# A four-tap filter on TensorE: from shifted 128-row products to products on 32-row groups, four at once, with the weights built in one operation

## The chip, the cores and the metric

One core of one Trainium2 chip. The metric is the time of one execution on the device in microseconds. The kernel before ran three times: 268.84, 270.32 and 270.63 us, median 270.32. The engines are called by the profile's names: PE (TensorE matmuls), PEld (its weight loads), DVE (VectorE), ACT (ScalarE), POOL (GpSimd) and SP (the queue that issues nearly all transfers).

## The reference

Two independent layers whose outputs stand side by side. Layer A (columns 0 to 639 of the output) is the one that the change touches; its first step is a causal filter of four taps over the 2048 positions, one filter for each of the 640 channels, and a product with v:

```python
k_pad = jnp.pad(k, ((0, 0), (ks - 1, 0), (0, 0)))
for t in range(ks):                       # ks = 4
    k_shift = k_shift + k_pad[:, t:t + S, :] * shift_k[:, ks - 1 - t][None, None, :]
kv = k_shift * v
...
y_f = kv_f * kf_f[None, :, :, :]          # a long convolution with ssm_k, by FFT
y = irfft2(y_f)[:S] + kv * ssm_D
return q * y
```

Layer B is an attention of 32 heads of 20 over four segments of 512, with a memory carried from segment to segment: projections of x by wq, wk and wv, softmax inside the segment, a linear term from the memory, and a projection by wo. All inputs are bf16.

## The kernel before

Layer A goes by slices of 128 channels: `conv(dp)` for dp 0 to 4. Its long convolution is a Fourier transform written as matmuls (`spectrum`, with the table Wf), complex products on DVE (`product`) and the inverse as matmuls (`inverse`, with Wi). Layer B goes by eight units, a segment's half of the heads each: `project(u)` makes keys, queries and values, `attend(u)` fills blocks of logits (matmuls on 32-row groups, one head per group and PSUM bank, then two exponentials on ACT over two banks each, into the tile ET), multiplies by the values and divides.

`short_filter` (lines 476 to 528) makes k_shift * v of one slice. A transposing DMA brings k as kr, channels on partitions and positions along the row (line 492). For each of the four banks b the filter is a sum of matmuls into one PSUM bank: the stationary operand is kr read at every eighth position, 128 channels x 128 positions, and the moving operand is a piece of skd, which holds for each tap a diagonal matrix of that tap's weights. The result has positions on partitions and channels along the row, as `spectrum` wants it, and one DVE multiply per bank puts v on it (line 527, tile vt). There are two variants:

- dp 0 to 2 (lines 519 to 524): 128x128 diagonals, 7 matmuls a bank, for the distances 0, 1, -1, 2, -2, 3, -3, of 512 down to 128 columns.
- dp 3 and 4 (`TAP2 = (3, 4)`, lines 512 to 518): 64 channels with two taps each on the 128 rows, which needs copies of kr shifted by two positions. Three SBUF-to-SBUF transfers make them (lines 493 to 498, tiles kb and kr); then 10 matmuls a bank, of 128 or 64 columns.

The weights skd are built in the constructor (lines 349 to 360): the taps are brought to the right partitions by 12 tiny matmuls (lines 341 to 347), and since `SKA` names all five slices, ACT then multiplies an identity by each tap, four instructions a slice, twenty in all.

Nothing here is issued in the order of the Python text. Every call is recorded as an operation (`Recorder.add`); a stored permutation of all operations, `ORDER`, says in which order they are issued (`issue`, line 252), `BASE` gives each PSUM group its first bank of eight, and `EVICT` says for each eviction from PSUM whether DVE ("1") or ACT ("0") does it. They are made beforehand with prices as in `price` (line 198). Each engine works through its own share of the order strictly in sequence. Line 261, from which every instruction is issued, is therefore the line that the profile gives for all of them; a tile's name tells them apart (ps is PSUM, skd and kr are the filter, ET the exponentials, vt the product with v).

Of the kernel before, what the change touches and what calls it, by code (L numbers as in the profile page):

```python
# [12 lines left out]
BF16_NP = ml_dtypes.bfloat16  # L13
bf16 = mybir.dt.bfloat16
f32 = mybir.dt.float32
# [11 lines left out]
KPAD = 16  # L27
# [242 lines left out]
class Layer:  # L270
    def __init__(self, ctx, tc, A_q, A_k, A_v, A_shift_k, A_ssm_k, A_ssm_D, B_x, B_wq, B_wk, B_wv, B_wo, B_beta, out):
# [52 lines left out]
        parts = [sel_np, ml_np, mr_np, np.concatenate([np.eye(64)] * 2).astype(BF16_NP), maskbd_np, eps_np.view(BF16_NP), step_np]  # L324
# [5 lines left out]
        sel, ml, mr, id2, mb, eps, step = [pack[:, int(a):int(b)] for a, b in zip(at, at[1:])]  # L330
# [6 lines left out]
        self.taps = o2[:, 640:720].bitcast(f32).rearrange("p (n c) -> p n c", c=5) if NP else c.tile([128, 8, 5], f32, name="taps")[:]  # L337
        g = self.taps_g = self.group(1, "taps")
        tp = g.ap[:, 0, 0:40].rearrange("p (n c) -> p n c", c=5)
        sk4 = skr.rearrange("c (f p s l) -> c f s p l", f=2, p=64, s=2)  # L340
        with rec.one():
            for f in range(2):
                for l in range(2):
                    for s in range(2):
                        nc.tensor.matmul(tp[64 * s:64 * s + 64, 2 * f + l, :], lhsT=sk4[:, f, s ^ f, :, l], rhs=self.ident[0:5, 0:5], start=True, stop=True, grp=g)
            for t in range(4):
                nc.tensor.matmul(tp[:, 4 + t, :], lhsT=skr.rearrange("c (d t) -> c d t", t=4)[:, :, t], rhs=self.ident[0:5, 0:5], start=True, stop=True, grp=g)
        self.evict(self.taps, tp, g)
        self.skd = []
        for dp in range(5):  # L350
            rec.key = ("skd", dp)
            n, k, eye = (256, 64, id2) if dp in TAP2 else (512, 128, self.ident[:])
            t = c.tile([128, n], bf16, name=f"skd{dp}")
            at = 0 if dp in TAP2 else 4
            if dp in SKA:
                for i in range(4):
                    nc.scalar.activation(out=t[:, k * i:k * i + k], in_=eye, func=ACTF.Copy, scale=self.taps[:, at + i, dp:dp + 1])
            else:
                nc.vector.tensor_tensor(out=t[:].rearrange("p (t d) -> p t d", t=4), in0=eye[:, None, :].to_broadcast([128, 4, k]), in1=self.taps[:, at:at + 4, dp, None].to_broadcast([128, 4, k]), op=ALU.mult)
            self.skd.append(t[:])  # L360
# [5 lines left out]
        self.kr = c.tile([128, KPAD + S], bf16, name="kr")  # L366
# [8 lines left out]
        nc.gpsimd.memset(self.kr[:, 0:KPAD], 0.0)  # L375
        self.kb = c.tile([128, KPAD + S], bf16, name="kb")
        nc.gpsimd.memset(self.kb[:, 0:KPAD], 0.0)
# [66 lines left out]
    def conv(self, dp):  # L444
# [5 lines left out]
        def key(*k):  # L450
            rec.key = ("A", dp) + k
# [24 lines left out]
        def short_filter():  # L476
            key("lk")
            kr = self.kr
# [23 lines left out]
            if dp in TAP2:  # L502
                skd2 = self.skd[dp].rearrange("p (f l d) -> p f l d", f=2, l=2)
            else:
                skd = self.skd[dp].rearrange("p (t d) -> p t d", t=4)
            for b in range(4):
                key("ks", b)
                if b % KSW == 0:
                    g = self.group(KSW, "ks")
                ps = g.ap[:, b % KSW, :]  # L510
                first = KPAD + 1024 * (b // 2) + 4 * (b % 2)
                if dp in TAP2:
                    with rec.one():
                        for m in (0, 2, -1, 1, 3):
                            for f, kx in ((0, kr), (1, self.kb)):
                                c0, c1 = max(0, m), min(4, m + 2)
                                nc.tensor.matmul(ps.rearrange("p (c d) -> p c d", d=128)[:, c0:c1, 64 * f:64 * f + 64], lhsT=kx[:, first + m:first + m + 1017:8],
                                                 rhs=skd2[:, f, c0 - m:c1 - m, :], start=(m == 0 and f == 0), stop=(m == 3), grp=g, skip_group_check=True)
                else:
                  with rec.one():  # L520
                    for n, dl in enumerate((0, 1, -1, 2, -2, 3, -3)):
                        c0, c1 = max(0, dl), min(4, 4 + dl)
                        nc.tensor.matmul(ps[:, 128 * c0:128 * c1], lhsT=kr[:, first + dl:first + dl + 1017:8], rhs=skd[:, c0 - dl:c1 - dl, :],
                                         start=(n == 0), stop=(n == 6), grp=g, skip_group_check=True)
                if b % KSW == KSW - 1:
                    some = vt[:, b + 1 - KSW:b + 1].rearrange("p b c d -> p b (c d)")
                    V.tensor_tensor(out=some, in0=g.ap, in1=some, op=ALU.mult, grp=g)
# [388 lines left out]
    def project_out(self, s):  # L916
# [41 lines left out]
        for t in range(4):  # L958
# [29 lines left out]
KSW, IW = 1, 1  # L988
NP = 0
SKA = (0, 1, 2, 3, 4)  # L990
KQV, QN = 0, 4
TAP2 = (3, 4)
EVICT = ("10100001110000001000000010000000000000000000000000000000000000100000000000001000010001001010100110100000000000000000110000000000000010000000"
         "000000000101000100100100000000000000010000001100001000000000000000000000010110010000100")
KQW, FW, WW = 1, 1, 1
ORDER = r"""
c-jrtgMttW5Czb=Gk0=rwrjI(+um&3wry{=YqM?Jwr#$5zT#w+Y?57aNKVNmxh0R}l_(NXTtrGs6^SI}q@v`L>Jn9=NgOF7p(MXlmGV+nk_aWQR+7{bAQdE|RFeV{Sqe%KEhI&?uv8XEKCPs6rKXsuRMxIiTWU#W
Ni5MNro@oa8cWJ(eyt%v(p?H@LP;gXw2qY3G*Vw`YC~x*^`x9;k=D{uifcCs(gxB<+DZ!vEw!|<l$177TboKh=^^bTtyIx;Qc-(J9c?9bwU0EBdfH6VOM5A$9i^(ql_FAH3Tl6;p*^Lr_LjcVLCWhO=_CWBn8cG|
l3cpT2<a@brG(Vi1d>RGNJA|u4K%C_mN7C=hRY~PDPd%s43)7mTB>OyEupJ*yo{6yQb>b!gErRcx<}S%d?~3-wTaHry|PjlX$tA4$t076lL|UfR%vscB$H)|?2`~(tW#yPY?AI;N@mDL-7l?lnrzbPazK`751p$s
rL`{AHabt6X<PlJEwsHJm6qB;=W9EiC0pg7bkd&MOBZNIJtlp1wj7qux=jwrHr=jAq__6bwc16y>Kxgj+hv^|my6O*Pe`!r)M2_=FUeI|p$m1m_SY>sK(EPMiDM&lr^K~gx>YaBX_+VEb-rAYcy>mX%Pxs(6Lp|2  # L1000
kli{#<J%57FN1WCuGif%Mx$A38>fq8uP&6NwnZ+;GTo<R^{gzG!MaSA>p3~5`!%Jdv7tIdPs&n>k5rb-qT6vjpp$f(PS;a1QV(i)nXEDFzKqsUn%Ex7bD5$`WQNYv>oQeu$qKn4H|4e**2j{>?#L{CDR<?NX0{`m
!B)#reIT<n0UpU~c_nM)jjWVJc2QqQR768Uq_DTLN)jQXWwQ11L@wz&$zoUZvOblha!sE}R@)$JB{9-lcDt&lb)CGIVV1)_N-`uzY&)w@bhw?-50V5S@>DlUPCKE`^ppl7DRS8-IjK`@gq_o=Hqr)KbX?FBh#<H1
yymvg5(9ZHrp2<<_#$bM#|GIqiHSS<Q19wjNrUV9NMqr#-q4$x4!884=CeMCjkkJVze|35pg&~1^|v^9r|<QZCbzU!!0yQ}iHiZ26|XhWe##roh<JFeza^bzLT3Dx43f>p+8>!<FSMY&)C86dAM}g<laKmU$5=uO
g-@CVpS7fY(}_0DfYO#8-!(J@KeUu(fFV03SxV$U8B2wqTGkZPtgscbB38+!8&S?8ps4jjWgBJ1tcp1zA}2;$aVuf7E!YNIE_A{Wt7>5|%Vt;}6h}3yZecOgCR+*Au-qt$APa|@79Qm-5{hAt<;7g9VEIrUg;5rz
QPE0bp1ri%))xVoZ-G+BDxe(dS`jR?0jOuStPB=eJ1d3yRuBQ~U_&iG8rV8pZ0)VJ^+!WnZ(t!Tu`rCxwicUhOxeOJVyO*8SjJ%#4na$+gk`qeMxd2d!3vAYMm7kQF%-iv5-V+i4Mt;YYE8`eTZf}6R#`QWG1=V4
U>us+Sj6H6tAUL+9^n`n9j%jvXJ-qs1YB)vY^`;%C@@RNuJ%{E8LczA+g9sg|Fox7M=$Gb+pLd?ZMXRB&P42Mn=A<va|$+FKXZ#j*cR)CP!@xCFqFG3G?TI)doTinFpSB$$EKn`yJG_O+78=i1+d?0;(-0piHOKR
*2Y1L#va&ZJFN@i@{mPmEhOU^i^qHDz&^Z-!`2gZ(3L58&d%B;>&trR#*`d|RJ>xBZ5q<B7mnHt)W<P9V#n=-rDjLY#7V1*(Ku!2tv9Bl0WMlZYY68gq-AKkV4>I*H!K~S;-=lQ!3?nG7{c2Y+3uKHW8AgLxM%Hn
)goDYUbFjXg!IhJ>z0uN*pv5dEHiOAnxGj@+hWYZ1AAnT?THQIQ=5%B2xFr-kip2pUR;9VoQs9%#0;E=wFqmYxdJ1&2wC~edb2Yh+Ip<R7`8)pF2xf(w`^R7hse!w+<<3zfc6;Ayd24ie2Ud*fjnG^HCTm7e2yG!
gPhF8`MANB$j1c;L4HnV7q-F_w#6k}Mr%x^djW>>f}GAG6feZ0gim8(7Go6Kh#7og#aW4=eI{REGfJ>BH=zpuvLv^lBevotI-mx__&5Gz5P$GHtFk74avQ4gJxg-}w__H|uq?~*Bdhb3T|q6DVtIbx96rJhd}19|
U@))ZG3K&1>vA?Dcmp<MBhF(*?!+}T<~O`S6E<aie!(vMVLgVk>-dhhXvRg{jfNi4!`oMUwi{^97Hr8@T+Hykg!8!vk-Rl;;<bITM*h*%7jgk3`&Yh#`7N~JC+x#gwq<*#f3nwjhbSK8x3Qe-xEB#@89R7XU(cGp  # L1010
9~&6L6?~7+*vMn}fK{yJoA?o{xsnI4mSH`bH}i0Q5NmiGwLQAOvwdvt@9hWnv%VkTQT)Ua1b7VJ%q`r?ZQRZV9@7uwAY=I<9O7ZN^&Q;FuNK=|czoZ@Jv@QE{DseK=dN-5H;(Wx{@@D(^dwsPQ6A$dgwns3*#F_p
{}GDkyLcM^40?)@HHp8qq#oDLK((uzez4O#i{tF#)Dt|zvka>z+0D-}wAS-5dY(NziiX#4n!qD!R6U2D9zoCJ7ZZ6Tji$-`0u%ZV>*W{O*?%*-CikBf=$CkzSD3<6`EN_<S9y(ptc~aQ>x`+ry^mi+L2v3Yw6Ul5
# [80 lines left out]
```

## Time and profile before

| | before |
|---|---|
| runs | 268.84, 270.32, 270.63 us |
| span of the profiled execution (first to last instruction) | 266.3 us |
| its own time | between 2.5 and 4.3 us above the span, by the three runs |
| instructions | 10034 |
| granted TensorE clock | 1.000 |
| PE busy | 257.8 us, 97% |
| DVE busy | 247.1 us, 93% |
| ACT busy | 248.8 us, 93% |
| DMA | 41.84 MB, 157 GB/s |

The trace gives the span of the one execution that it records, and no time around it. "Busy" is the union of the records of an engine; a record includes the tail of an instruction, so two records that follow each other overlap, and a merged row of the timeline (start, length, engine, operation, output and inputs, shape, count) is longer than the distance to the next row by one tail. A stretch row gives, for each engine, busy time and in brackets the number of instructions, in the order PE, PEld, DVE, ACT, POOL, then the granted clock, the share of the DMA engines and GB/s. A group row gives the count, the busy time, the mean length of one in ns, and the idle time ahead of them. A tile's row gives shortest, median and longest in ns.

### The profile page before, as it was taken

How to read it: one execution, taken by the hardware profiler on the slowest of the kernel's cores; microseconds unless marked ns; L12 is line 12 of the kernel's file. 1: busy time of each engine (PE TensorE's matmuls, PEld its weight loads, DVE VectorE, ACT ScalarE, POOL GpSimd, SP SyncE). 2: the span in 40 equal slices, each digit the busy share in tenths (PEclk: the TensorE clock that was granted, in tenths of full speed). 3: DMA queues.
4: the chain of work that ended last, by engine and by line, in shares of the span. 5: the costliest groups of instructions: out<-in, count | busy, mean ns of one | idle time of the engine just before them, and what ended most of it. 6: DMA issues, size and time to landing. Idle time of an engine off the chain costs nothing.

```text
span 266.3 us, 10034 instructions
## 1 busy us (share of the span) xinstructions
PE 257.8 (97%) x4323; PEld 193.0 (72%) x4323; DVE 247.1 (93%) x387; ACT 248.8 (93%) x392; POOL 7.6 (3%) x20
## 2 busy tenths in 40 slices
PE   7999999999999999999999999999999999988994
PEld 3788678778777778877767777778776876665871
DVE  0599999999999999999999999999999999999971
ACT  2878999999999999999999999999999999999953
POOL 8300000000000000000000000000000000000000
PEclk9999999999999999999999999999999999999999
DMA  7999898999989797996999699958990099345034
GB/s 217 292 214 218 197 180 187 126 233 205 172 200 175 142 180 162 173 154 126 154 173 201 164 185 182 211 107 113 181 186 3 29 158 149 87 108 128 28 66 116
DMA packets 126604, 41.84 MB, mean 157 GB/s; under 512 B 114107, under 2 KB 125376, under 8 KB 126432
## 3 DMA queue, kind: packets, MB, share of 16 engines
q1 hardware_dynamic: 126416, 41.07, 80.1%
q8 instruction: 34, 0.56, 0.9%
q0 software_dynamic: 144, 0.13, 0.1%
q14 instruction: 10, 0.08, 0.1%
HBM read 11.96 MB, written 5.24 MB: 65 GB/s over the span
## 4 chain that ended last, share of the span: by engine, by line
PE 62%; ACT 28%; DVE 5%; issue 2%; DMA 1%; POOL 0%; DVEq 0%; ACTq 0%; POOLq 0%
PE ps L261 62%; ACT ET L261 19%; ACT F L261 3%; ACT KQ L261 1%; ACT PP L261 1%; DMA qabs<-in_A_shift_k_dram 1%; ACT Va L261 1%; DVE vt L261 1%; ACT outb L261 1%; DVE Y L261 1%; DVE Kh L261 1%; ACT qabs L261 1%; DVE pq L261 0%; ACT xT L261 0%; DVE o L261 0%
## 5 line engine op out<-in xcount | busy, mean ns | idle before, releaser
L261 ACT ACTIVATE ET<-ps 128x1024 bf16<-128x1024 f32 x160 | 162.6, 1122 | 0.4 <-PE ps L261 0.2
L261 PEld LDWEIGHTS <-xT 128*128 128x128 bf16 x640 | 57.3, 98 | 27.8 <-issue 6.8
L261 PE MATMUL ps<-wqkv,xT 128*128 128x320 bf16 x480 | 77.0, 299 | 0.4
L261 ACT CAST F<-ps 128x512 bf16<-128x512 f32 x72 | 43.3, 686 | 0.9 <-DVE F L261 0.8
L261 PE MATMUL ps<-Va,ET 128*128 128x21 bf16 x1280 | 41.8, 173 | 0.0
L261 PEld LDWEIGHTS <-ET 128*128 128x128 bf16 x1280 | 39.1, 96 | 2.1 <-issue 1.0
L261 PE MATMUL ps<-KQT 32*128 32x128 bf16 (+3 forms) x896 | 35.7, 239 | 0.3
L261 PEld LDWEIGHTS <-Wf 128*128 128x128 bf16 x320 | 29.8, 98 | 6.1 <-issue 1.3
L261 ACT CAST KQ<-ps 128x320 bf16<-128x320 f32 x54 | 25.5, 513 | 2.4 <-PE ps L261 2.3
L261 PE MATMUL ps<-wo,xT 128*128 128x320 bf16 (+2 forms) x160 | 25.5, 299 | 1.3 <-ACT ET L261 1.3
L261 PEld LDWEIGHTS <-KQT 32*128 32x128 bf16 (+1 forms) x896 | 16.1, 92 | 9.9 <-issue 8.2
L261 PE MATMUL ps<-kT,Wf 128*128 128x256 bf16 x160 | 21.8, 273 | 0.1
L261 PE MATMUL ps<-vt,Wf 128*128 128x256 bf16 x160 | 21.2, 273 | 0.0
L261 PE MATMUL ps<-Y,Wi 128*128 128x256 bf16 x160 | 20.8, 273 | 0.0
L261 DVE TENSOR_TENSOR o<-ps,rr 128x640 bf16<-128x640 f32 x24 | 19.7, 819 | 0.4
L261 DVE TENSOR_TENSOR Y<-Y,pq 128x2048 bf16<-128x2048 bf16 (+1 forms) x20 | 18.6, 937 | 0.0
L261 PE MATMUL ps<-Mbd,PqT 128*128 128x84 bf16 x96 | 18.3, 203 | 0.1
L261 DVE TENSOR_TENSOR pq<-Xh,Kh 128x2048 bf16<-128x2048 bf16 x15 | 18.2, 1215 | 0.0
L261 PE MATMUL ps<-skd,kr 128*128 128x128 bf16 (+4 forms) x124 | 17.9, 270 | 0.0
L261 PEld LDWEIGHTS <-kr 128*128 128x128 bf16 x124 | 15.6, 147 | 2.5 <-issue 0.8
L261 PEld LDWEIGHTS <-Wi 128*128 128x128 bf16 x160 | 14.8, 98 | 2.5 <-issue 0.6
L261 ACT ACTIVATE PP<-KQ 128x1280 bf16<-128x1280 bf16 x12 | 15.9, 1361 | 0.0
(87 smaller groups left out, 355.6 us busy)
## 6 DMA issues: line engine op xcount, KB each, us to landing
vt<-in_A_v_dram SPq DMA_DIRECT2D x10, 256.0 KB
pq<-in_A_q_dram SPq DMA_DIRECT2D x10, 256.0 KB
kT<-kT SPq DMA_DIRECT2D x32, 64.0 KB
out_dram<-pq SPq DMA_DIRECT2D x8, 256.0 KB
out_dram<-outb SPq DMA_DIRECT2D x12, 160.0 KB
Wf<-c_wf SPq DMA_DIRECT2D x4, 256.0 KB
Wi<-c_wi SPq DMA_DIRECT2D x1, 1024.0 KB
kb<-kr SPq DMA_DIRECT2D x4, 256.0 KB
```

Source lines behind the costliest of these rows:

```text
L261: f(*[fix(a) for a in args], **{k: fix(v) for k, v in kw.items()})
```

## The change

The filter is one variant for all five slices. The 128 channels are cut into four quarters of 32, each on its own 32 partitions and so on its own group of 32 rows of the array. For each half a of the positions and each of eleven distances m there are four matmuls, one per quarter r, with 32 rows, 128 columns of kr as weights and 32 to 128 columns of skd; quarter r writes bank r of four, so that the four of one step touch four row groups and four banks. That is 2 x 11 x 4 = 88 matmuls a slice, recorded as one operation with a stated price of 1260 ns (`KSD`). The four banks are two groups of two, and two DVE multiplies of 1024 elements a row put v on them.

The shifted copies (kb, the transfers "lc") are gone. The weights are one tile of 5 x 4 x 32 columns, made by one DVE operation from a stacked 32x32 identity and the taps, whose tiny matmuls are 4 instead of 12. kr has two buffers in place of one.

`ORDER`, `BASE` and `EVICT` are new throughout: 1455 operations for 1505, in 461 groups for 471. Read out, the new order has the filter of dp 0 as the 30th operation on PE (its four parts were 36th to 40th); the load of kr as 12th on SP behind two of the four loads of Wf (13th, behind all four); the loads of kr for dp 2, 3 and 4 at places 37, 49 and 92 on SP (47, 69 and 105). Evictions on DVE are 34 in both: 9 of keys and queries (10), 3 of values (1), 12 of the output projection (9), 7 of spectra (8), 2 of transposed filter (2), 1 of x (1), none of the bound (1), of transposed outputs (1) or the taps (1).

```diff
-        parts = [sel_np, ml_np, mr_np, np.concatenate([np.eye(64)] * 2).astype(BF16_NP), maskbd_np, eps_np.view(BF16_NP), step_np]
+        parts = [sel_np, ml_np, mr_np, np.concatenate([np.eye(32)] * 4).astype(BF16_NP), maskbd_np, eps_np.view(BF16_NP), step_np]
...
         with rec.one():
-            for f in range(2):
-                for l in range(2):
-                    for s in range(2):
-                        nc.tensor.matmul(tp[64 * s:64 * s + 64, 2 * f + l, :], lhsT=sk4[:, f, s ^ f, :, l], rhs=self.ident[0:5, 0:5], start=True, stop=True, grp=g)
             for t in range(4):
-                nc.tensor.matmul(tp[:, 4 + t, :], lhsT=skr.rearrange("c (d t) -> c d t", t=4)[:, :, t], rhs=self.ident[0:5, 0:5], start=True, stop=True, grp=g)
+                nc.tensor.matmul(tp[:, t, :], lhsT=skr.rearrange("c (d t) -> c d t", t=4)[:, :, t], rhs=self.ident[0:5, 0:5], start=True, stop=True, grp=g)
         self.evict(self.taps, tp, g)
-        self.skd = []
-        for dp in range(5):
-            rec.key = ("skd", dp)
-            n, k, eye = (256, 64, id2) if dp in TAP2 else (512, 128, self.ident[:])
-            t = c.tile([128, n], bf16, name=f"skd{dp}")
-            at = 0 if dp in TAP2 else 4
-            if dp in SKA:
-                for i in range(4):
-                    nc.scalar.activation(out=t[:, k * i:k * i + k], in_=eye, func=ACTF.Copy, scale=self.taps[:, at + i, dp:dp + 1])
...
+        self.skd = c.tile([128, 5, 4, 32], bf16, name="skd")
+        rec.key = ("skd",)
+        nc.vector.tensor_tensor(out=self.skd[:], in0=eye[:, None, None, :].to_broadcast([128, 5, 4, 32]),
+                                in1=self.taps.rearrange("p t c -> p c t")[:, :, :, None].to_broadcast([128, 5, 4, 32]), op=ALU.mult)
...
-        self.kr = c.tile([128, KPAD + S], bf16, name="kr")
+        self.kr = [c.tile([128, KPAD + S], bf16, name=f"kr{i}") for i in range(2)]
...
-            kr = self.kr
+            kr = self.kr[dp % 2]
...
-            if dp in TAP2:
-                key("lc")
-                q = self.queue("lc", dp)
-                q.dma_start(out=self.kb[64:128, KPAD:KPAD + S], in_=kr[64:128, KPAD:KPAD + S])
-                q.dma_start(out=self.kb[0:64, KPAD:KPAD + S], in_=kr[64:128, KPAD - 2:KPAD + S - 2])
-                q.dma_start(out=kr[64:128, KPAD:KPAD + S], in_=kr[0:64, KPAD - 2:KPAD + S - 2])
...
-            for b in range(4):
...
-                    V.tensor_tensor(out=some, in0=g.ap, in1=some, op=ALU.mult, grp=g)
+            key("ks")
+            gs = [self.group(2, "ks") for _ in range(2)]
+            with rec.one(KSD):
+                for a in range(2):
+                    for m in (0, 1, 2, 3, 4, 5, 6, 7, -1, -2, -3):
+                        c0, c1 = max(0, m), min(8, m + 4)
+                        for r in range(4):
+                            rows = slice(32 * r, 32 * r + 32)
+                            first = KPAD + 1024 * a + m
+                            nc.tensor.matmul(gs[r // 2].ap[:, r % 2, 256 * a + 32 * c0:256 * a + 32 * c1], lhsT=kr[rows, first:first + 1017:8], rhs=self.skd[rows, dp, c0 - m:c1 - m, :],
+                                             start=(a == 0 and m == 0), stop=(a == 1 and m == -3), grp=gs[r // 2], skip_group_check=True)
+            for i in range(2):
+                key("kv", i)
+                some = vt[:].rearrange("p b c (r d) -> p r (b c) d", d=32)[:, 2 * i:2 * i + 2]
+                V.tensor_tensor(out=some, in0=gs[i].ap.rearrange("p r (x d) -> p r x d", d=32), in1=some, op=ALU.mult, grp=gs[i])
...
-KSW, IW = 1, 1
+IW = 1
...
-SKA = (0, 1, 2, 3, 4)
-TAP2 = (3, 4)
+KSD = 1260
```

More of the change, by code (lines that the diff above doesn't have):

```diff
@@ L329, in __init__ @@
         nc.gpsimd.dma_start(out=pack[:], in_=self.real.inline_tensor(np.ascontiguousarray(np.concatenate(parts, axis=1)), name="c_pack").ap())
-        sel, ml, mr, id2, mb, eps, step = [pack[:, int(a):int(b)] for a, b in zip(at, at[1:])]
+        sel, ml, mr, eye, mb, eps, step = [pack[:, int(a):int(b)] for a, b in zip(at, at[1:])]
         self.sel, self.mleft, self.mright = sel, ml, mr
@@ L374, in __init__ @@
         nc.gpsimd.memset(self.PP[:, 1, :, :, DH + 1:DH + 2], 1.0)
-        nc.gpsimd.memset(self.kr[:, 0:KPAD], 0.0)
-        self.kb = c.tile([128, KPAD + S], bf16, name="kb")
-        nc.gpsimd.memset(self.kb[:, 0:KPAD], 0.0)
+        for i in range(2):
+            nc.gpsimd.memset(self.kr[i][:, 0:KPAD], 0.0)
         self.Va = [c.tile([128, 4, 16, VW], bf16, name=f"Va{i}") for i in range(2)]
@@ L501, in short_filter @@
             self.halves(self.queue("lv", dp), vt, self.v, dsl)
[L502 to L505, printed above, removed]
-            for b in range(4):
[L507 to L526, printed above, removed]
-                    V.tensor_tensor(out=some, in0=g.ap, in1=some, op=ALU.mult, grp=g)
@@ L528, in short_filter @@
+            for i in range(2):
+                key("kv", i)
+                some = vt[:].rearrange("p b c (r d) -> p r (b c) d", d=32)[:, 2 * i:2 * i + 2]
+                V.tensor_tensor(out=some, in0=gs[i].ap.rearrange("p r (x d) -> p r x d", d=32), in1=some, op=ALU.mult, grp=gs[i])
             return vt
@@ L1000 @@
[L1000 to L1012, printed above, removed]
```

43 lines of the change are left out of this document (26 added, 17 removed).

## The prediction

> **What bounds the kernel now.** I read the page's busy times and slices first, then the chain of waits, then busy time by stretch, then the timeline around one filter.
>
> ```profile
> PE 257.8 (97%) x4323; PEld 193.0 (72%) x4323; DVE 247.1 (93%) x387; ACT 248.8 (93%) x392; POOL 7.6 (3%) x20
> ...
> PE 62%; ACT 28%; DVE 5%; issue 2%; DMA 1%; POOL 0%; DVEq 0%; ACTq 0%; POOLq 0%
> ```
> ```profile
> 6.18 0.21 DVE taps L261
> 6.39 0.02 issue
> 6.42 0.40 ACT skd L261
> 6.82 0.59 ACT xT L261
> 7.41 0.05 issue
> 7.45 44.03 PE ps L261 x556
> ...
> 132.14 69.08 PE ps L261 x1243
> ```
> ```profile
> 0.00:10.00 10.00, 7.93 (x58) 4.53 (x59) 1.75 (x4) 4.29 (x9) 7.59 (x20) 1.00 0.81 240
> 10.00:20.00 10.00, 10.00 (x93) 8.47 (x92) 8.64 (x18) 7.37 (x17) 0.00 (x0) 1.00 1.05 242
> 20.00:250.00 230.00, 227.20 (x3969) 170.92 (x3968) 228.43 (x352) 228.43 (x356) 0.00 (x0) 1.00 0.84 156
> 250.00:266.30 16.30, 12.71 (x209) 9.13 (x207) 8.29 (x16) 8.71 (x13) 0.00 (x0) 1.00 0.29 74
> ```
> The chain names PE for 62% of the span, which by itself would say: what PE saves, the kernel saves. The stretches say otherwise. Between 20 and 250 us three engines have no room: PE is busy 227.2 of 230, VectorE (DVE, third pair) and ScalarE (ACT, fourth) 228.4 each. The chain follows PE because PE is seldom stopped; it doesn't show that the other two could go faster. VectorE is idle 1.6 us there, and its idle time lies at the ends: 8.3 us in the first ten, 1.4 in the next ten, 8.0 in the last sixteen.
>
> **TensorE (PE): what goes and what comes.** Slices dp 0 to 2 make each of four banks with 7 matmuls, dp 3 and 4 with 10:
> ```profile
> 17.30 1.93 PE L261 MATMUL ps<-skd,kr 128*128 128x512 bf16 x14
> 19.06 0.84 PE L261 MATMUL ps<-wqkv,xT 128*128 128x320 bf16 x5
> ...
> 115.76 0.85 PE L261 MATMUL ps<-wqkv,xT 128*128 128x320 bf16 x5
> 116.45 0.22 PE L261 MATMUL ps<-skd,kr 128*128 128x128 bf16 x1
> ...
> 117.04 0.25 PE L261 MATMUL ps<-skd,kr 128*128 128x128 bf16 x1
> ```
> Two banks take 19.06 - 17.30 = 1.76 us, so a slice takes 3.52 and three take 10.6. One bank of dp 3 takes 117.04 - 116.45 = 0.59, a slice 2.36, both 4.7. Removed: 15.3 us.
>
> Added: per slice 2 halves x 11 steps x 4 row groups = 88 matmuls on 32 rows. The 32-row matmuls of the attention blocks show what such a step costs:
> ```profile
> 30.82 1.11 PE L261 MATMUL ps<-wqkv,xT 128*128 128x320 bf16 x7
> 31.86 0.38 PE L261 MATMUL ps<-pack 32*128 32x128 bf16 x16
> 32.08 0.39 PE L261 MATMUL ps<-KQT 32*128 32x128 bf16 x16
> 32.45 0.84 PE L261 MATMUL ps<-wqkv,xT 128*128 128x320 bf16 x5
> ```
> ```profile
> L261 PEld LDWEIGHTS <-kr 128*128 128x128 bf16 x124 | 15.6, 147 | 2.5 <-issue 0.8
> ...
> L261 PEld LDWEIGHTS <-KQT 32*128 32x128 bf16 x512 | 8.7, 93 | 0.0
> ```
> Sixteen matmuls from 31.86 to 32.08 are 0.055 us for four, so four row groups do run at once. What these rows don't show is the new weight: kr is read at every eighth element, and such a load lasts 147 ns against 93 for a packed one. The ten matmuls of dp 3 load the same strided weights, 0.59 / 10 = 0.059 us each, though their columns alone (1024, at the 0.88 us that a bank with 2048 columns takes) would need 0.44: there the load sets the pace. I take 0.06 us for a step of four, the loads of four row groups side by side as the packed ones go: 22 x 0.06 = 1.32 us a slice, 6.6 for five. Bounds: 0.055 a step, as above (6.1), or no overlap of strided loads at all (a rival below).
>
> Changing between whole array and row groups costs too. Seven projections of 0.138 (0.69 / 5) fill 0.97 of the 1.04 us to 31.86: 0.07 to enter; four steps of 0.055 end at 32.30, the next starts at 32.45: 0.15 to leave; 0.22 a round trip. Five filters are five trips at most. The stored order, counted before and after, holds 173 and 180 changes, 3.5 trips more: 0.8 us. PE's sum: -15.3 + 6.6 + 0.8 = **-7.9 us**.
>
> [...]
>
> **ScalarE (ACT).** The filter's weights leave it, twenty instructions, and one small eviction (taps) comes:
> ```profile
> 11.42 1.27 ACT L261 ACTIVATE skd<-ident,taps 128x128 bf16<-128x128 bf16 x4
> ```
> ```profile
> L261 ACT ACTIVATE skd<-ident,taps x12: 364/396/587, 6.4 to 29.6; 128x128 bf16<-128x128 bf16 x12
> L261 ACT ACTIVATE skd<-pack,taps x8: 306/359/563, 7.3 to 107.8; 128x64 bf16<-128x64 bf16 x8
> ```
> The records overlap by their tails; at the spacing of four, (1.27 - 0.40) / 3 = 0.29, twenty are at most 5.8 us of work. The twelve large ones lie before 30 us, where ACT isn't full (4.29 and 7.37 of the first two tens), so it buys little; only the 0.40 us that stands on the chain at 6.42 counts: **-0.4**.
>
> **VectorE (DVE).** Twenty multiplies of 512 from PSUM become ten of 1024, and one 640-element product builds the weights:
> ```profile
> 14.36 0.48 DVE L261 CAST KQ<-ps 128x320 bf16<-128x320 f32 x1
> 14.76 0.68 DVE L261 CAST F<-ps 128x512 bf16<-128x512 f32 x1
> ...
> 20.12 2.48 DVE L261 TENSOR_TENSOR vt<-ps,vt 128x512 bf16<-128x512 f32 x4
> ...
> 253.68 0.83 DVE L261 TENSOR_TENSOR o<-ps,rr 128x640 bf16<-128x640 f32 x1
> 254.42 0.68 DVE L261 CAST xT<-ps 128x512 bf16<-128x512 f32 x1
> 255.02 0.68 DVE L261 TENSOR_TENSOR pq<-ps,pq 128x512 bf16<-128x512 f32 x1
> ```
> A 512 goes every 0.60, a 640 every 0.74, so 1.09 ns an element, and a 1024 takes 0.60 + 512 x 1.09 = 1.16 us, between 1.12 (0.13 for 128, by rounding) and 1.20 (two of 512). Twenty at 0.60 less ten at 1.16: 0.4 us saved. The product, 0.74, falls in the first 20 us, where VectorE idles 9.6; without that cover it would cost 0.74. The evictions in EVICT are 34 on VectorE before and after. Their kinds shift: of 320 columns three more (0.40 each, 14.36 to 14.76), of 512 two fewer, the taps gone: 1.2 - 1.2 - 0.2 = -0.2. In all **-0.6 us**.
>
> **Queues, copies, new order.** Six copies that shift kr and kb leave SP and the DMA rings.
> ```profile
> L261 SPq DMA_DIRECT2D kb<-kr x4: 526/594/1135, 95.0 to 141.7; - x4
> L261 SPq DMA_DIRECT2D kr<-kr x2: 464/482/499, 110.0 to 148.1; - x2
> ```
> ```profile
> 4.64 2.09 SPq L261 DMA_DIRECT2D Wf<-c_wf  x4
> 6.78 6.39 SPq L261 DMA_TRANSPOSE kr<-in_A_k_dram  x1
> ```
> The filters behind them start at once (116.45 follows the projection by its own 0.69), so their data came in time and they buy nothing. The second kr lets the loads of slices 2 to 4 stand earlier on SP (place 47 becomes 37, 69 becomes 49, 105 becomes 92), past the transposes of keys and queries. Should a transpose come late by such an issue, an attention block waits up to 6.4 us; I take 0, as these loads are moved ahead and none is added. At the start two of the four Wf loads now stand behind the 6.39 us of the kr issue: issued after 12.7 instead of by 6.7. The first spectrum on PE is now behind the filter, so I take 0, up to 2 us lost.
>
> **The sum.** The sum is made against 266.3 us of span and the 4.0 that lie between it and the median, 270.32 (the three runs, 268.84 to 270.63, put 2.5 to 4.3 around it). VectorE can end earlier by its own 0.6, by 0.4 at the start, and by what it now waits for the other two: 1.6 idle between 20 and 250, and small waits hidden by record tails, of which I count 0.3. PE's 7.9 us cannot go further than that, as VectorE has no more to give. 270.3 - 0.6 - 0.4 - 1.9 = **267.4 us**, 1.1% faster; with 0 to 2.5 for the waits its own range is 266.8 to 269.3.
>
> **The rivals.**
> PE's saving comes through whole: 270.3 - 7.9 = 262.4. For it: 62% of the chain. Against it: VectorE's 228.4 of 230; it needs some 5 us of waits hidden in overlapping records. A record's tail hides up to 0.08 in each (0.68 long, 0.60 apart), so it isn't excluded.
>
> Nothing arrives: the new order's own stalls eat the 1.9 and VectorE ends where it did, 269.5 to 270.3. For it: three full engines, so an order that saves on two of them keeps the third's end.
>
> Slower, by four banks. The filter holds four of eight banks from its first matmul until VectorE's second multiply. Place: each filter, behind VectorE's backlog. Held: 1.32 + 0.22 + 2 x 1.16 = 3.9 us at least; and while PE waits for its fourth bank, the projections and spectra queued behind the filter wait with it. An attention block needs four banks (two activations), so one block at a time fits, and ACT waits for its refill instead of having the next one ready.
> ```profile
> 242.90 4.89 ACT L261 ACTIVATE ET<-ps 128x1024 bf16<-128x1024 f32 x5
> ```
> ```profile
> L261 ACT ACTIVATE ET<-ps 128x1024 bf16<-128x1024 f32 x160 | 162.6, 1122 | 0.4 <-PE ps L261 0.2
> ```
> Two activations take 1.9 us ((4.89 - 1.12) / 4 = 0.94 each), a block on PE 0.59 (31.86 to 32.45); two blocks in the hold lose 1.2 to 1.5 us, five filters up to 7.5: 270.3 - 2.9 + 7.5 = 274.9. It decides above 0.6 us a filter (2.9 / 5). Against it: the order was written for these groups, and filters can stand where other work has its banks.
>
> Slower, by loads that don't overlap, that is, not four at once: 88 x 0.06 = 5.3 us a slice, 26.4 for five, PE 26.4 + 0.8 - 15.3 = 11.9 more, 282.2. It decides above (15.3 - 0.8) / 110 = 0.13 us a step. Against it: the 147 ns of a strided load differ from the packed one's 93 by 54 only, and packed ones in four row groups do overlap.
>
> **How the numbers follow.** One per cent, 2.7 us, is about what a measurement of this kernel can tell. Forecast 0.45 (0.27 of it beyond 1%), PE's whole saving 0.22, nothing arrives 0.16, four banks 0.11, loads one by one 0.06. Faster: 0.27 + 0.22 = 0.49; same: 0.18 + 0.16 = 0.34; slower: 0.11 + 0.06 = 0.17. The range reaches from 261.9 (the step's lower bound, 6.1 for 6.6, under PE's whole saving) to 274.5, so that the lost start, 2 us on any of these, and most of the banks' cost lie in it; the loads one by one stay out.
>
> **What would show it.** Right: filter blocks of about 1.35 us, 22 steps of 0.06; ten multiplies spaced 1.16 or less; no skd on ACT; VectorE busy over 228 of 230 between 20 and 250, with the slack on PE, whose 227.2 of that stretch falls by several us. Wrong: VectorE's count of busy time falls with the span by over 3 us (then records hid waits); steps at 0.2 us; ACT idle beside the filters; or a first spectrum that waits for Wf.

## The result and the profile after

The changed kernel takes 287.49 us (median of four runs, 286.79 to 289.37) against 270.48 for the kernel before on the same chip: a ratio of 1.0676, interval 1.0612 to 1.0739, 17 us slower where 2.9 faster was forecast. The profiled execution has a span of 285.8 us. Times of experiments are medians of the runs in the chip's faster state (e2, e8, e11, e14 and e17 have one run each left out; with it e11's median is 286.4 us), and the profiles of e14 and e17, which were taken in the slower one, aren't read.

The busy times, the clock by slice and the chain, from the page:

```profile
PE 255.4 (89%) x4590; PEld 186.0 (65%) x4591; DVE 248.9 (87%) x378; ACT 246.2 (86%) x372; POOL 8.0 (3%) x20
...
PEclk9999999999899999999999999959999999999999
...
PE 26%; ACT 20%; DMA 4%; issue 4%; DVE 1%; ACTq 0%; DVEq 0%
```

Busy time by stretch (PE, PEld, DVE, ACT, POOL, then the granted clock, the DMA share and GB/s):

```profile
0.00:10.00 10.00, 8.08 (x52) 4.38 (x53) 1.24 (x3) 4.59 (x10) 5.54 (x16) 1.00 0.79 224
10.00:20.00 10.00, 8.33 (x149) 6.49 (x148) 7.40 (x11) 6.17 (x12) 2.44 (x4) 1.00 1.00 206
20.00:250.00 230.00, 209.29 (x3822) 153.92 (x3822) 211.98 (x321) 208.33 (x317) 0.00 (x0) 0.98 0.80 144
250.00:285.80 35.80, 29.74 (x569) 21.22 (x569) 28.24 (x46) 27.14 (x36) 0.00 (x0) 0.99 0.32 82
```

Over the whole span each engine has about as much to do as before: PE 255.4 us for 257.8, ACT 246.2 for 248.8, DVE 248.9 for 247.1. What changed is that all three stand still. Between 20 and 250 us ACT was busy 228.4 and is now 208.3, 20.1 us less; the span grew by 285.8 - 266.3 = 19.5. With the work unchanged the two must go together, so this says that the engines wait, not why. The chain no longer runs along PE alone (62% before, 26% now), and DMA's share of it went from 1% to 4%.

The filter itself came out as forecast. The timeline at the first and at the fourth filter:

```profile
15.85 1.53 PE L261 MATMUL ps<-skd,kr 32*128 32x128 bf16 x88 [0.90 <-DMA kr<-in_A_k_dram]
...
17.32 1.92 PE L261 MATMUL ps<-kT,Wf 128*128 128x256 bf16 x16
```
```profile
130.79 2.08 ACT L261 ACTIVATE ET<-ps 128x1024 bf16<-128x1024 f32 x2
...
131.08 1.54 PE L261 MATMUL ps<-skd,kr 32*128 32x128 bf16 x88 [0.73 <-ACT KQ L261]
...
132.61 1.41 ACT L261 ACTIVATE PP<-KQ 128x1280 bf16<-128x1280 bf16 x1
132.69 2.35 DVE L261 TENSOR_TENSOR vt<-ps,vt 128x1024 bf16<-128x1024 f32 x2 [0.27 <-issue]
```

From 15.85 to the next matmul on the whole array at 17.32 are 1.47 us; less the 0.15 to leave the mode, 22 steps take 1.32, 0.06 each. The second multiply starts 2.35 - 1.22 = 1.13 us after the first.

What the engines wait for now (total us, times, longest):

```profile
ACT F L261 <- PE ps L261: 12.7, 7, 6.0
PE ps L261 <- ACT ET L261: 8.0, 22, 1.0
PE ps L261 <- DMA KQT<-qabs: 6.9, 2, 4.8
...
DVE pq L261 <- DMA pq<-in_A_q_dram: 4.9, 1, 4.9
...
PE ps L261 <- DVE vt L261: 1.1, 1, 1.1
```

In the kernel before, no engine waits for a transfer this long after the start. The largest after the start, at 65 us, seen from the queue that issues and from the engines that wait:

```profile
61.81 4.34 SPq L261 DMA_TRANSPOSE kr<-in_A_k_dram  x1
66.19 0.59 SPq L261 DMA_DIRECT2D pq<-in_A_q_dram  x1
66.83 0.66 SPq L261 DMA_DIRECT2D kT<-kT  x1
67.59 0.59 SPq L261 DMA_DIRECT2D KQT<-qabs  x1
```
```profile
70.17 0.69 DVE L261 TENSOR_TENSOR pq<-ps,pq 128x512 bf16<-128x512 f32 x1 [4.91 <-DMA pq<-in_A_q_dram]
...
70.48 1.01 PE L261 MATMUL ps<-kT,Wf 128*128 128x256 bf16 x4 [4.78 <-DMA KQT<-qabs]
```

The kr load of slice 3, which isn't used before 131 us, holds SP for 4.34 us. Half of the q of slice 0 and the bound rows (KQT<-qabs) stand behind it, are issued at 66.19 and 67.59, and DVE and PE stand still until 70.2 and 70.5. PE then pays a second time:

```profile
68.00:70.00 2.00, 0.00 (x0) 0.00 (x0) 0.00 (x0) 1.31 (x2) 0.00 (x0) 1.00 0.93 210
70.00:71.00 1.00, 0.52 (x3) 0.42 (x4) 0.83 (x2) 0.00 (x0) 0.00 (x0) 0.54 0.91 168
71.00:73.00 2.00, 2.00 (x15) 1.43 (x14) 2.00 (x3) 0.00 (x0) 0.00 (x0) 0.50 0.58 133
```

The TensorE clock granted after the pause is 0.50, half of full speed, from 70.08 to 73.49 us. Over the run it is 0.981 where it was 1.000.

### The profile page after: what moved, and what is told of

It reads as the page before. It is cut to its first block, busy times and chain, and to the rows that moved or that the text cites. A ratio compares the mean times of both kernels' runs of the same rounds, so it can differ in the third digit from the quotient of the medians.

```text
span 285.8 us, 10545 instructions
## 1 busy us (share of the span) xinstructions
PE 255.4 (89%) x4590; PEld 186.0 (65%) x4591; DVE 248.9 (87%) x378; ACT 246.2 (86%) x372; POOL 8.0 (3%) x20
## 4 chain that ended last, share of the span: by engine, by line
PE 26%; ACT 20%; DMA 4%; issue 4%; DVE 1%; ACTq 0%; DVEq 0%
PE ps L261 26%; ACT ET L261 13%; ACT F L261 2%; DMA xT<-in_B_x_dram 2%; DMA KQT<-KQ 2%; ACT KQ L261 1%; ACT PP L261 1%; ACT Va L261 1%; ACT outb L261 1%; DVE vt L261 0%; ACT qabs L261 0%; DVE outb L261 0%; DVE Y L261 0%; ACTq L261 0%; DVEq L261 0%
## 5 line engine op out<-in xcount | busy, mean ns | idle before, releaser
L261 ACT ACTIVATE ET<-ps 128x1024 bf16<-128x1024 f32 x160 | 159.4, 1093 | 5.8 <-PE ps L261 5.7
L261 ACT CAST F<-ps 128x512 bf16<-128x512 f32 x73 | 42.2, 651 | 14.1 <-PE ps L261 12.7
L261 PEld LDWEIGHTS <-ET 128*128 128x128 bf16 x1280 | 40.1, 97 | 3.7 <-issue 2.4
L261 PE MATMUL ps<-KQT 32*128 32x128 bf16 (+3 forms) x896 | 34.1, 240 | 3.9 <-DMA KQT<-qabs 2.1
L261 ACT CAST KQ<-ps 128x320 bf16<-128x320 f32 x55 | 26.1, 495 | 5.0 <-PE ps L261 2.0
L261 PE MATMUL ps<-kT,Wf 128*128 128x256 bf16 x160 | 22.7, 276 | 6.7 <-DMA KQT<-qabs 4.8
L261 PE MATMUL ps<-vt,Wf 128*128 128x256 bf16 x160 | 22.7, 276 | 1.8 <-ACT KQ L261 1.2
L261 DVE TENSOR_TENSOR pq<-ps,pq 128x512 bf16<-128x512 f32 x20 | 13.7, 687 | 5.7 <-DMA pq<-in_A_q_dram 4.9
L261 PEld LDWEIGHTS <-Wi 128*128 128x128 bf16 x160 | 15.3, 100 | 4.0 <-issue 1.8
L261 PE MATMUL ps<-pack 32*128 32x128 bf16 (+1 forms) x512 | 13.4, 212 | 2.0 <-ACT ET L261 1.8
```

The source lines that it names most:

```text
L261: f(*[fix(a) for a in args], **{k: fix(v) for k, v in kw.items()})
```

## The experiments

The first theory: the filter is good, and the new order puts bulk transfers ahead of small urgent ones on SP. The rivals: the order of the compute engines is itself worse; or four banks held at once make the attention wait. Each run's ratio, with its 95% interval, is to the kernel before on the same chip, which took 268.3 to 268.9 us there.

**e1 and e2: SP's order alone.** All other engines' orders, banks and evictions are those of the changed kernel.

```diff
 SP's place of the transposing kr load   (e1; counted from 1, as above)
-slice 2: 37   slice 3: 49   slice 4: 92
+slice 2: 48   slice 3: 72   slice 4: 107
 SP's 195 transfers                      (e2)
+all in a new order, by when each is first needed
```

> The changed kernel; on SP's queue alone the three transposing kr loads of slices 2 to 4 stand behind the same transfers as in the kernel before. Theory (the new stored order puts bulk loads ahead of the attention's transposes on SP): the 4.94 us wait for KQT<-qabs at 65 us and the DMA waits at 85 and 144 us go, and the time falls by 5 to 12 us, to 275 to 282 us. Rival (the new order of the compute engines is itself the worse one, transfers apart): within 2 us of the changed kernel's 287.5. Rival (four banks held by the filter): the same, no change.

> The changed kernel with the orders of PE, DVE, ACT and POOL kept, and all of SP's 195 transfers put in a new order by when they are needed. Theory (SP's order): nearly all of the 17 us lost comes back, 266 to 273 us, and PE's waits for KQT<-qabs, xT<-in_B_x and pq<-in_A_q shrink below 3 us together. Rival (order of the compute engines): 280 us or more, PE's idle time now ended by DVE and ACT instead of by DMA. Rival (four banks): 280 us or more, with PE idle in the first step of each filter.

Measured: e1 282.79 us, ratio 1.0534 (1.0480 to 1.0587); e2 281.41 us, 1.0438 (1.0360 to 1.0517). The waits of e1 for the same two transfers:

```profile
PE ps L261 <- DMA KQT<-qabs: 3.2, 2, 2.0
DVE pq L261 <- DMA pq<-in_A_q_dram: 1.6, 1, 1.6
```

The named waits shrink as they should (4.9 to 1.6 for q), and the loss shrinks from 17.0 us to 14.1 and 12.7. But e1 was expected at 282 or less and e2 at 273 or less: SP's order is part of the cause, not the cause.

**e3 and e4: both kernels without the bulk.** Layer A's loads of slices 2 to 4 are left out, everything else keeps its order.

```diff
-              nc.sync.dma_start_transpose(out=kr[...], in_=self.k[:, dsl])
+              if dp < 2:
+                nc.sync.dma_start_transpose(out=kr[...], in_=self.k[:, dsl])
 (the same for v, q and the long filter's transposes and their reshuffle)
```

> The changed kernel without layer A's loads of k, v, q and the long filter in slices 2 to 4 (45 transfers; these slices work on what slice 0 and 1 left, so the output of layer A is another); every other instruction in its order. Theory: with the bulk gone the attention's transposes come in time and the time is that of the compute engines, 262 to 268 us, less than the old kernel without the same loads by 2 to 8 us. Rival (order of the compute engines): 278 us or more, longer than the old kernel without these loads by 8 us or more.

> The kernel before without the same 45 loads of slices 2 to 4 (output of layer A another, as in the run beside it). Both theories: it hardly waits for DMA, so 267 to 271 us, within 2 us of the kernel before.

Measured: e3 278.19 us, ratio 1.0349 (1.0301 to 1.0397); e4 268.66 us, 0.9992 (0.9965 to 1.0019). The stretch from 0 to 50 and from 50 to 250 us of e3, then of e4:

```profile
0.00:50.00 50.00, 43.83 (x569) 30.65 (x570) 35.15 (x52) 34.09 (x64) 7.39 (x20) 1.00 0.98 208
50.00:250.00 200.00, 189.07 (x3617) 139.95 (x3614) 193.11 (x296) 194.35 (x288) 0.00 (x0) 0.99 0.57 101
```
```profile
0.00:50.00 50.00, 48.45 (x582) 36.20 (x583) 40.14 (x63) 40.03 (x83) 7.58 (x20) 1.00 0.94 207
50.00:250.00 200.00, 197.16 (x3533) 147.62 (x3532) 198.51 (x310) 199.85 (x298) 0.00 (x0) 1.00 0.60 112
```

These 45 transfers cost the old kernel nothing (0.1 us) and the new one 17.0 - 9.5 = 7.5 us. That leaves 9.5 us that they don't explain, and in its place ACT is busy 5.9 us less before 50 us and 5.5 us less after. e3 met the number of the rival. The first theory holds for somewhat under half of the loss.

**e5 to e7: the new filter in other orders.** e5 puts it into the old stored order, each block at the place of one of the four old ones; e6 moves the instructions around it to fit; e7 keeps the changed kernel's instructions, banks and evictions and orders all queues anew.

```diff
 order of PE, one slice   (e5)
-... ks0 ... ks1 ... ks2 ... ks3 ...
+... ks (four banks) ...
 order of DVE, one slice
-... kv0 ... kv1 ... kv2 ... kv3 ...
+... kv0, kv1 (128 x 1024 each) ...
```

> The new filter (weights by one operation, products on 32 rows, four banks, two multiplies of 1.22 us) put into the old stored order: every other instruction of every engine where the kernel before has it, also SP's transfers, banks and evictions; each filter block stands at the place of one of the four old ones. Theory (the filter is good, the new order is what costs): 262 to 270 us. Rival (four banks held at once make the attention wait): 274 to 282 us, with PE and ACT idle just ahead of and within each filter.

> As the run beside it, but with the instructions around the filters moved to fit the four-bank block. Theory: 262 to 268 us. Rival (four banks): 270 us or more even so. Rival (DVE and ACT have no room, so PE's saving has nowhere to go): 266 to 270 us.

> The changed kernel with the same instructions, banks and evictions, and the order of every engine and of SP's transfers searched anew. Theory that orders alone are at fault: 265 to 271 us, so 17 to 22 us under the changed kernel. Rival (the filter's four banks or its transfers cost it in any order): 275 us or more.

Measured: e5 284.61 us, ratio 1.0586 (1.0533 to 1.0638); e6 287.16 us, 1.0692 (1.0648 to 1.0737); e7 285.71 us, 1.0629 (1.0577 to 1.0682). e6 and e7 are where the four-bank rival put them (270 or more, 275 or more); e5 is slower than both of its ranges (the rival had 274 to 282). The new filter is slow in these orders too, so the new stored order alone isn't what makes it slow. One filter of e5:

```profile
76.23 1.53 PE L261 MATMUL ps<-skd,kr 32*128 32x128 bf16 x86 [0.63 <-ACT ET L261]
...
77.82 2.36 DVE L261 TENSOR_TENSOR vt<-ps,vt 128x1024 bf16<-128x1024 f32 x2 [0.30 <-issue]
...
80.23 0.62 PE L261 MATMUL ps<-KQT 21*128 21x384 bf16 x8 [2.47 <-DVE vt L261]
...
80.89 1.94 ACT L261 ACTIVATE ET<-ps 128x1024 bf16<-128x1024 f32 x2 [2.88 <-PE ps L261]
```

PE waits for ACT to clear banks, makes its 86 products, then waits 2.47 us for the multiplies to give the banks back before it can write the next attention block; ACT, out of blocks, waits 2.88. A drain ahead of the filter, a refill behind it. This is one filter; over the run PE waits 8.7 us for these multiplies, in six places (the row stands with e9 below). e6 and e7 leave open whether some better order exists: neither beats the kernel before, and neither is clearly below the changed one.

**e8: less PE work in the old kernel.**

```diff
-                    for n, dl in enumerate((0, 1, -1, 2, -2, 3, -3)):
+                    for n, dl in enumerate((0,)):
```

> The kernel before with only the middle product of the seven in the old filters of slices 0 to 2 (12 of 16 column shares left out, so about 2.64 of 3.52 us in each of three filters, 7.9 us of PE in all, and the output of layer A is another); no order, bank or transfer is changed. If PE set the time (the rival of the whole saving): 262 to 263 us. If DVE and ACT are as full as PE, so that PE's saving alone goes nowhere: 267 to 270 us.

Measured: 270.54 us, ratio 1.0053 (1.0018 to 1.0088). The products left out are worth 7.9 us of PE, the very size of the forecast saving (PE's busy time between 20 and 250 us, which counts a slower clock too, fell from 227.2 to 221.9), and the kernel is if anything slower, a little above the 267 to 270 expected. The clock goes with that: two runs with a granted clock of 0.997 and 1.000 took 268.2 us, the others, at 0.985 to 0.994, took 269.4 to 272.1.

**e9 to e11: which part of the filter.** e9 is the old filter, its products and weights unchanged, run as one block into four banks with two large multiplies; e10 and e11 are the new products, one and two channel quarters at a time.

```diff
 e9, in the old kernel and its order
-KSW, IW = 1, 1
+KSW, IW = 2, 1    (and the four blocks of a slice one behind the other)
 e10, e11: the new products in the old order
-for r in range(4): products of a step into banks 0..3
+one group of one bank per quarter (e10), of two banks per pair of quarters (e11)
```

> The kernel before with its old products and weights, but the four of a slice run one behind the other into four banks at once, read by two multiplies of 128 x 1024 as in the change; nothing else is moved. Theory (the four banks held at once, with the multiplies that release them, make the attention wait, and a waiting PE loses its clock): 278 to 290 us, though no new product is in it. Rival (the new products on 32 rows, or their transfers, cost the time): within 3 us of the kernel before, 267 to 272 us.

> The new products and weights in the old order, but one channel quarter at a time into one bank, in the places and banks of the old four, with four multiplies of 128 x 512. Theory (four banks): most of the loss is gone, 268 to 276 us: the products now follow each other on one row group (PE about as long as the old filter) and change the array's mode 20 times more, up to 4.4 us at 0.22. Rival (the new products themselves): 280 us or more, as with four banks in the same order.

> The new products and weights in the old order, two channel quarters at a time into two banks, each pair released by its own multiply of 128 x 1024. Theory (four banks): between one bank and four, 272 to 281 us. Rival (the new products): 280 us or more. Also read here: the pace of a step of two row groups, about 0.03 us if each product costs the same, 0.06 us if a step costs the same.

Measured: e9 281.83 us, ratio 1.0471 (1.0405 to 1.0537); e10 291.66 us, 1.0845 (1.0766 to 1.0924); e11 285.16 us, 1.0605 (1.0509 to 1.0702). e9 is where its theory put it; e10 (268 to 276) and e11 (272 to 281) are misses. One filter of e9, and the waits of PE for the filter's multiplies in e5 and then in e9 (total us, times, longest):

```profile
76.20 3.70 PE L261 MATMUL ps<-skd,kr 128*128 128x512 bf16 x28
...
76.96 1.26 ACT L261 ACTIVATE ET<-ps 128x1024 bf16<-128x1024 f32 x1
...
79.84 0.38 PE L261 MATMUL ps<-pack 32*128 32x128 bf16 x16
...
80.48 1.94 ACT L261 ACTIVATE ET<-ps 128x1024 bf16<-128x1024 f32 x2 [2.25 <-PE ps L261]
```
```profile
PE ps L261 <- DVE vt L261: 8.7, 6, 2.5
```
```profile
PE ps L261 <- DVE vt L261: 3.0, 2, 1.7
```

With no new product in it, gathering the old filter into one block of four banks costs 13.6 us, 2.7 a slice. ACT waits 2.25 us here, but not quite as in e5: PE starts the next attention block at 79.84, right behind the filter's last product, so what ACT waits for in this slice is the length of the gathered block on PE, 3.64 us, and not the multiplies that give the banks back. For those PE waits in two places of e9 only, 3.0 us in all. So e9 shows the cost of the gathered four-bank block; how much of it is the banks and how much the block's length on PE, no run separates. e10 was meant as the other side of this and failed at it, because its cost was mis-sized. A stretch of filter products in e10 and one in e11:

```profile
45.22 1.35 PE L261 MATMUL ps<-skd,kr 32*128 32x128 bf16 x19
46.37 0.28 PE L261 MATMUL ps<-KQT 21*128 21x256 bf16 x2
```
```profile
38.24 1.43 PE L261 MATMUL ps<-skd,kr 32*128 32x128 bf16 x40
39.45 0.28 PE L261 MATMUL ps<-KQT 21*128 21x256 bf16 x2
```

Nineteen products on one row group take 46.37 - 45.22 = 1.15 us, 0.061 each; forty on two take 1.21, 0.061 for a step of two; 0.060 for a step of four above. A step costs the same for one, two or four row groups. So e10 gives PE 4 x 22 x 0.061 = 5.4 us a slice, 27 for five where the old filter had 15.3, and 4.4 more for mode changes: its 23 us say nothing on banks. e11's products take 2 x 22 x 0.061 x 5 = 13.4, with 2.2 of mode changes about the old filter's 15.3, so its 17 us aren't PE's work. They may be the pairs of banks or the clock (0.958); the run doesn't tell them apart.

**e12: the weights alone.** The old kernel, its weights by five multiplies on DVE in place of twenty activations on ACT.

```diff
-SKA = (0, 1, 2, 3, 4)
+SKA = ()
```

> The kernel before with its filter weights built by five multiplies on DVE in place of 20 activations on ACT, in the same places; nothing else. This is the change's step on the weights, nearly alone. By the prediction (0.4 us of ACT on a path of the start) and by each theory: within 1.5 us of the kernel before, 267 to 270.5 us.

Measured: 268.71 us, ratio 1.0014 (0.9985 to 1.0042). No effect clear of the noise, though ACT's busy time fell from 248.8 to 244.6 us.

**e13 and e14: the products again, by the clock and in the new order.**

```diff
 e13, ahead of each of e11's blocks
+for n in range(3): matmul(bank n % 2, lhsT=kr (128 x 128), rhs=kr (512 columns), start=True)
 e14, in the changed kernel
-22 steps x 4 products on 32 rows
+the old seven products on 128 rows, into the same four banks
```

> The run with two banks (286.4 us, seven stretches of 3.41 us at half clock in its profiled execution) with three more products of 128 x 128 on 512 columns put ahead of each of its ten blocks, into the same banks, overwritten by the block: 30 x 0.21 = 6.4 us more PE work and nothing else. [...] Rival (the clock follows PE's waits alone, or has no part in the loss): 288 to 293 us, with the clock as it was.

> The changed kernel with its order, banks, transfers and two multiplies kept, but the old products (seven on 128 rows for each of four banks, 3.5 us a slice in place of 1.3) in the filter; slice 4 takes the weights of slice 3, so its output is another. If the order and the four banks make the loss: within 4 us of the changed kernel, 284 to 292 us, though PE has 10 us more to do. If the products on 32 rows make it, by the clock: 275 to 282 us, and no stretch at half clock behind a filter. If PE sets the time in the new order: 295 us or more.

Measured: e13 289.91 us, ratio 1.0753 (1.0668 to 1.0838), granted clock 0.965; e14 287.74 us, 1.0687 (1.0590 to 1.0784). e13 lies where its rival put it (288 to 293 us): with thirty products of 512 columns more the clock of the profiled runs rose from 0.958 to 0.965 only, and the time went up by 4 to 5 us. e14 speaks against the products as the cause: in the new order the old ones, 11.0 us longer on PE (5 x 3.52 less 6.6), give the time of the changed kernel within 2 us (0.3 by the medians, 1.9 by what each lies over the kernel before). The loss is in the order with its transfers and four-bank blocks, whichever products fill them.

**e15 and e16: is it the time that the multiplies hold the banks?**

```diff
-V.tensor_tensor(out=some, in0=g.ap, in1=some, op=ALU.mult)
+V.tensor_tensor(out=some[first 64 of 512], in0=g.ap[...], in1=some[...], op=ALU.mult)
```

> The changed kernel without the 45 loads of slices 2 to 4 (278.2 us) and with the two multiplies that read the filter's banks cut to 64 of each 512 columns (10.6 us of DVE less in all; the output of layer A is another): the four banks come back about 2 us earlier in each slice. If the time that the multiplies hold the banks is what is left of the loss: the time falls by 6 us or more beyond what the same cut gives the old kernel, to its own time or below. If it is the order of the compute engines: it falls by no more than the old kernel does.

> The old kernel without the 45 loads of slices 2 to 4 (268.7 us) and with its twenty multiplies cut to 64 of 512 columns (DVE about 9 us less in all; the output of layer A is another). If DVE sets the time: 259 to 262 us. If ACT and PE are as full: 266 to 269 us.

Measured: e15 277.72 us, ratio 1.0305 (1.0243 to 1.0366), 0.5 us below e3 (1.2 by the ratios); e16 268.03 us, 0.9953 (0.9922 to 0.9984), 0.6 below e4 (1.0 by the ratios). The time that the multiplies hold the banks isn't what is left in the new order, and relieving DVE alone brought only 0.6 to 1.0 us in the old one. The busy times of e16 agree with that:

```profile
20.00:250.00 230.00, 226.48 (x3966) 170.89 (x3968) 220.95 (x351) 228.63 (x356) 0.00 (x0) 1.00 0.64 121
```

DVE's busy time falls from 228.4 to 221.0 of 230; ACT's stays at 228.6 and PE's at 226.5.

**e17 and e18: is it ACT alone?**

```diff
-nc.scalar.activation(out=ET[...], in_=gs[i].ap, func=ACTF.Exp)
+nc.scalar.activation(out=ET[... 0:480], in_=gs[i].ap[:, :, 0:480], func=ACTF.Exp)   (e17, u > 0)
+the cuts of e8 and e16 as well                                                   (e18)
```

> The kernel before with 140 of its 160 exponentials cut from 1024 to 960 columns (those of all heads' blocks but the first; the output of layer B is another): at 1.114 us for 1024 columns some 0.06 us each, 8 to 9 us of ACT in all; nothing else. If ACT alone sets the time: 259 to 262 us. If ACT, DVE and PE are equally full from 20 to 250 us (228.4, 228.4 and 227.2 us busy of 230): the time falls by no more than DVE's spare, 0 to 3 us, so 265 to 269 us.

> The kernel before with all three cuts at once: the exponentials (8 to 9 us of ACT), the twenty filter multiplies cut to 64 of 512 columns (9 us of DVE), and only the middle product in the old filters of slices 0 to 2 (7.9 us of PE); outputs are others. If the three engines are equally full: now the time falls by about what each was relieved of, 5 to 9 us, 259 to 263 us, though each cut alone brought nothing. If something else (transfers, the tail, waits between the engines) sets it: less than 3 us.

Measured: e17 267.70 us, ratio 0.9940 (0.9918 to 0.9963), 1.2 us less; e18 266.30 us, 0.9878 (0.9842 to 0.9914), 2.6 us less. e17 agrees with three equally full engines, e18 doesn't: with all three relieved (by their busy times over the span 7.4 us for PE, 8.2 for DVE and 4.6 for ACT, less than was meant) only 2.6 came. In e18 all three have gaps:

```profile
20.00:250.00 230.00, 221.19 (x3940) 164.69 (x3942) 221.81 (x355) 224.76 (x356) 0.00 (x0) 0.99 0.85 156
```

A likely reason, not tested: the cuts lie at different places (PE's and DVE's at the filters, ACT's at every block but the first), the orders are fixed, and each engine still waits for another's result where that isn't shorter.

## Why the prediction was wrong, point by point

The step that failed is the sum: it took what DVE is spared off the end and put at nothing what the change makes the engines wait for, the moved loads ("I take 0") and the filter's four banks. In their place the runs showed 7.5 us for the late transfers (e3 and e4) and 9.5 us more in the new order, of which the four-bank block is the likely but not the separated cause: in the old order it costs 13.6 us (e9).

**What bounds it: half right.** That PE's share of the chain (62%) overstates what PE can give was right: e8 took 7.9 us from PE and got nothing. That a saving on one of the three engines goes nowhere while the others are full was right for PE, DVE and ACT one at a time (e8, e16, e17). The prediction named DVE as the one that sets the end; DVE relieved alone moved the end by about 1 us (e16), and even the three together aren't a sum of busy times (e18). The 1.9 us of "waits that DVE has" were booked as a gain with no mechanism that would remove them; DVE's busy time in the stretch fell from 228.4 to 212.0.

**PE's term: right.** Block 1.32 us (measured 1.32), step 0.06 (0.060), multiplies 1.16 apart (1.13), no skd on ACT. PE's busy time fell by only 2.4 us, but the clock not granted (5.4 us, below) is in it. The 88 products of a block on four row groups took 1.32 us, 15 ns each. The rival of loads one by one is dead: a step costs as much with one row group (0.061 us, e10) as with four (0.060). The product that builds the weights takes longer than priced and lies, as said, in idle time:

```profile
L261 DVE TENSOR_TENSOR skd<-pack,taps x1: 1137/1137/1137, 12.7 to 12.7; 128x640 bf16<-128x640 bf16 x1
```

Against 0.74 for a 640 read from PSUM. ACT's -0.4 wasn't seen in e12 (+0.4; its interval, -0.4 to +1.1, just reaches it).

**Queues: failed.** "I take 0, as these loads are moved ahead and none is added." A load that is moved ahead moves everything else back. The 6.4 us named as a bound on one attention block was near (4.8), and I dropped it. e3 and e4 put the late bulk at 7.5 us; putting the three kr loads back returned 2.9 of it and all of SP's order 4.3 (17.0 less 14.1 and 12.7). The rest may be order that the search missed or competition for the rings; not separated. The start, where up to 2 us were named and 0 taken, has its part: PE waits 0.9 us for kr at 15.85 and 0.6 for Wf at 21.5, and even in e3 ACT is busy 5.9 us less in the first 50.

**The four banks: the right rival, dismissed.** The drain and refill of e5 is the mechanism that it described: the multiplies hold the banks, one attention block at a time fits, ACT waits for its refill. e9 shows ACT waiting behind the gathered block as well, there mostly for PE. The rival was priced at 1.2 to 1.5 us a slice, 7.5 in all, and given 0.11 because "the order was written for these groups, and filters can stand where other work has its banks". In the old order the gathered block costs 2.7 us a slice (e9), 3.2 with the new filter (e5), the clock's part (0.988 and 0.964) included. The new order avoids most of the direct wait (PE waits for the filter's multiplies once, 1.1 us, and ACT isn't stopped at the filter of 131 us above), but without late transfers it still stands 9.5 us behind (e3). What in it costs that, its start (about half by ACT's busy time), the blocks' places or the clock, stays open; the products (e14) and the length of the multiplies (e15) are unlikely.

**The clock: not in the prediction.** In the changed kernel the stops of PE of 4.8 us at 65.7 and of 1.6 at 185.6 come with a clock of 0.50, from 70.08 to 73.49 and from 186.14 to 192.96; the one of 2.1 at 34.3 doesn't (1.00 from 33 to 43 us). Its mean of 0.981 on 285.8 us is 285.8 x 0.019 = 5.4 us of full-speed PE time not granted, and the profiled run of every slow variant has some of it (e5 0.964, e10 0.953). How much of the 17 us that makes isn't separated. e2 hints at it: its one run at full clock took 278.2 us, those at 0.970 and 0.986 took 282.0 and 281.4. The changed kernel's four runs, 0.963 to 0.981, show no such order.

## What to carry to other kernels

When three engines are each full for most of the span, a saving on one of them is worth about nothing (ratios of 0.994 to 1.005 in e8, e16 and e17), so ask of such a change not what it saves but what it makes wait: here a filter gathered into four banks at once let the attention's stock of blocks run out, and loads moved ahead made small ones late. Cut one engine's work in the old kernel, leaving the order alone, before building the change: e8 would have told in one run that PE's saving goes nowhere. And of a load that is moved ahead on a queue, list what stands behind it and when that is needed; a transposing load that holds the queue for 4.34 us, as here, is a wait for everything behind it.

## What the runs showed of the hardware

**A step of 32-row products with these strided weights costs 0.06 us whether one, two or four row groups take part** (0.061 in e10, 0.061 in e11, 0.060 in the changed kernel, above). Of the banks the runs show the price of a gathered block of four in the old order, 13.6 us (e9) to 16.1 us (e5).

**The clock can halve while PE is busy.** In e10, whose filter products on one row group fill nine tenths of the slice from 79.4 to 86.6 us:

```profile
85.00:88.00 3.00, 3.00 (x67) 2.90 (x56) 3.00 (x6) 2.70 (x3) 0.00 (x0) 1.00 0.87 208
88.00:89.00 1.00, 1.00 (x10) 0.71 (x9) 1.00 (x3) 1.00 (x2) 0.00 (x0) 0.71 0.90 179
89.00:91.00 2.00, 2.00 (x12) 0.88 (x14) 2.00 (x4) 0.50 (x3) 0.00 (x0) 0.50 1.03 353
```

PE is busy 3.00 of 3.00 us, and the clock still falls to 0.50. e8 has a stretch at half clock that the kernel before doesn't have, though products were left out there and nothing else was changed: 0.76 from 76 to 77 us, 0.50 from 77 to 79 and 0.53 from 79 to 80, behind 3 us in which PE was busy 2.02; the kernel before is granted 1.00 from 74 to 84. In the changed kernel the two stretches last 3.41 and 6.82 us; the means of the windows put those of e10 and e8 at 3.4 and that of e5 from 78 to 85 us at 6.8 (estimates). What sets the half clock off isn't shown: it came at stops of PE of 4.8 and 1.6 us and not at one of 2.1, it came in e10 with no stop in the 3 us ahead, and with the thirty products added in e13 the mean was 0.965 for e11's 0.958.
